# Later maxima for the attention heads, and the weight conversion's integer word in PSUM

## The chip, the cores and the metric

The kernel runs on one core of one Trainium2 chip. The metric is the device time of one execution in microseconds. Three runs of the kernel before gave 982.65, 981.98 and 981.62 us, median 981.98 us. A trace of one execution, taken by the hardware profiler, is the source of every other time in this text. The engines are named as in the profile: PE (TensorE matmul), PEld (its weight load), DVE (VectorE), ACT (ScalarE), POOL (GpSimd), SP (the queue that issues most DMAs).

## The reference

Two layers, one behind the other. The first is attention in which a key counts for a query only if both fall into the same of 64 buckets; the second is a feed-forward layer over the 3072 tokens that the first returns.

```python
# q, k, v: (4, 8, 768, 64); proj: (64, 6)
q_bits = (einsum('bhsd,dk->bhsk', q, proj) > 0)
k_bits = (einsum('bhsd,dk->bhsk', k, proj) > 0)
q_bucket, k_bucket = sum(bits * 2 ** arange(6), -1)
mask   = q_bucket[:, :, :, None] == k_bucket[:, :, None, :]
scores = where(mask, q @ k.T / sqrt(64), -1e9)
attn   = exp(scores - max(scores, -1))
attn   = attn / (sum(attn, -1) + 1e-9)
x      = (attn @ v), as (3072, 512)
# w_in: (512, 2048), w_out: (2048, 512), both float64
h = x @ w_in
g = where(h >= 1, h, where(h <= -1, 0, (h + 1) ** 2 / 4))
out = g @ w_out
```

## The kernel before

The attention takes the 32 heads one after the other, in pairs that share their loads. A head is twelve **units**: two halves of 384 queries, times six blocks of 128 keys. The program writes out units 0 to 383 in one loop over `g`, and each engine works through its own instructions in the order in which that loop issues them; nothing is reordered. What is done beside the units (casts, conversions, transfers) stands in a table `tasks[g]` and is issued at the end of unit `g`. Where this text says "unit 14 of a head" it means unit 2 of the head behind it.

A unit issues, in this order:

- `s_unit(g)`: two matmuls (L371, L372) give the scores of a block, as a sum of a high and a low part, in one of four PSUM buffers of the pool `ps_s`. The mask and the query's maximum are part of the operands: rows 0 to 7 of the tiles `T1` and `T2` hold the bucket bits, and row 7 of one of them holds the negated maximum. ACT takes the exponential twice, once rounded for the matmul (`ph`, L380) and once in full (L385), into the same PSUM buffer, or for key blocks 0 and 3 into SBUF (`pf`).
- the reduction (`max_red`, L314) of the maximum step that was issued at the end of the unit before, if there was one.
- `lo_unit(g - 1)`: the low part `pl` = full minus rounded (L39), for key blocks 0 and 3 on POOL and otherwise on DVE.
- `pv_unit(g - 4)`: three matmuls with the values (L404 to L406) into one of two output banks, `obank[0]` for the first half of the queries and `obank[1]` for the second. Since they lag by four units, `obank[0]` is written in units 4 to 9 of a head and `obank[1]` in units 10 to 15. ACT then copies the bank to SBUF (`xs`, L412).
- a **maximum step** (`max_mm`, L310), if one is due: two matmuls of 128 queries against all keys of a later head, into the one buffer of the pool `ps_m`. Six of them make a head's maxima.
- the tasks of this unit.

The maxima of a head run two heads ahead of it. For heads 6 and up there is one step in each even unit 0, 2, ..., 10 of the head two before; for heads 0 to 5 a table `early` lists the units. When the six are done, `max_clamp` (L342, L344) makes flags and clamps, a PE transposition (`max_tr`, L349) turns the column to a row in `obank[1]`, and `max_put` copies it on ACT (`te`, L354) and sends it by DMA to its row of `T2` (L356) and to DRAM (L357).

In even heads the operands of the next pair but one are prepared: `cast_h` and `low_h` on POOL in units 0 to 3, `move` by DMA, the bucket bits by four matmuls for each half (`bits_mm`, L210) in units 7 (into `obank[1]`) and 11 (into `obank[0]`), a negation on ACT (L216) and a comparison on DVE (`bits_cmp`, L221) in the unit behind each, and `bits_scale` (L273) on POOL.

From head 3 to head 26 one piece of the feed-forward weights is converted in each head from float64 to a high and a low float32 part (`WeightSplit.steps`). Its parts and their units, counted from the head's unit 0:

| part | engine, line | unit |
|---|---|---|
| s0: load of the raw words `wraw` | SP, L62 | 0 |
| s1: square of the high word `wsq` (ACT), exponent and mantissa bits into the word `wa` (DVE) | L69, L70 | 7 |
| s2: sign bits into `wa` | DVE, L74 | 9 |
| s3: low bits into `wa` | DVE, L78 | 13 |
| s4: `wsq` = (square large enough) times `wa` | DVE, L82 | 15 |
| s5, s6, and the store of the sum for odd heads; a store alone for even ones | ACT L87, POOL L39, SP L95 | 17, 19, 21; 16 |

s2 to s4 read `wa`, and s2 and s3 write it in place. `wa` is an SBUF tile with one buffer. The feed-forward layer follows the attention and is not touched by the change.

Of the kernel before, what the change touches and what calls it, by code (L numbers as in the profile page):

```python
# [22 lines left out]
P = 128  # L23
# [18 lines left out]
class WeightSplit:  # L42
# [7 lines left out]
        nc.vector.memset(sc[:, 1:2], 29)  # L50
        self.sc = sc

    def steps(self, src, shape, hi, lo, cp, stage=None, low=None, keep=None):
        nc, n = self.nc, self.n
        st = {}

        def s0():
            st["raw"] = self.pool.tile([P, n, 2], I32, name="wraw")
            dst = st["raw"]
            if len(shape) == 4:  # L60
                dst = dst.rearrange("p (c f) t -> p c f t", c=shape[1])
            nc.sync.dma_start(out=dst, in_=src)  # L62

        def s1():
            raw = st["raw"]
            sq = st["sq"] = self.pool.tile([P, n], F32, name="wsq")
            a = st["a"] = self.pool.tile([P, n], I32, name="wa", bufs=1)
            high = raw[:, :, 1].bitcast(F32)
            nc.scalar.activation(out=sq, in_=high, func=AF.Square)  # L69
            nc.vector.tensor_scalar(out=a, in0=raw[:, :, 1], scalar1=0x07FFFFFF, scalar2=3,  # L70
                                    op0=ALU.bitwise_and, op1=ALU.logical_shift_left)

        def s2():
            nc.vector.scalar_tensor_tensor(out=st["a"], in0=st["raw"][:, :, 1], scalar=self.sc[:, 0:1],  # L74
                                           in1=st["a"], op0=ALU.bitwise_and, op1=ALU.bitwise_or)

        def s3():
            nc.vector.scalar_tensor_tensor(out=st["a"], in0=st["raw"][:, :, 0], scalar=self.sc[:, 1:2],  # L78
                                           in1=st["a"], op0=ALU.logical_shift_right, op1=ALU.bitwise_or)

        def s4():
            nc.vector.scalar_tensor_tensor(out=st["sq"], in0=st["sq"], scalar=WMIN2,  # L82
                                           in1=st["a"].bitcast(F32), op0=ALU.is_ge, op1=ALU.mult)
# [25 lines left out]
POOL_J = (0, 3)  # L109
PV_ORDER = (1, 2, 0, 4, 5, 3)  # L110
NU = 2 * NJ


def attention(ctx, tc, wst, T1, T2, qk, v, pj, cv, x_d, s_d, e_d, tasks, shared):
# [1 line left out]
    const = ctx.enter_context(tc.tile_pool(name="aconst", bufs=1))  # L116
    work = ctx.enter_context(tc.tile_pool(name="awork", bufs=2))
    small = ctx.enter_context(tc.tile_pool(name="asmall", bufs=2))
    shared["work"], shared["small"] = work, small
    ps_s = ctx.enter_context(tc.tile_pool(name="ps_s", bufs=4, space=PSUM))  # L120
    ps_o = ctx.enter_context(tc.tile_pool(name="ps_o", bufs=1, space=PSUM))
    ps_m = ctx.enter_context(tc.tile_pool(name="ps_m", bufs=1, space=PSUM))
# [221 lines left out]
        eng.tensor_scalar(out=nm[:, 0:NJ], in0=nm[:, 0:NJ], scalar1=CLAMP, scalar2=None,  # L344
                          op0=ALU.min)

    def max_tr(hd, bank):
        ps = mx[hd] = obank[bank]
        nc.tensor.transpose(out=ps[0:2 * NJ, 0:P], in_=nms.pop(hd), identity=ident)  # L349

    def max_put(hd):
# [40 lines left out]

    xss = {}

    def pv_unit(n):
        hd, hf, jj = n // NU, (n % NU) // NJ, n % NJ
        j = PV_ORDER[jj]
        pr, h = hd // 2, hd % 2
# [3 lines left out]
        wa = va[:, j, h:h + 2, :].rearrange("p g d -> p (g d)")  # L402
        wb = vb[:, j, h:h + 2, :].rearrange("p g d -> p (g d)")
        nc.tensor.matmul(out=o, lhsT=wa, rhs=ph, start=(jj == 0), stop=False)  # L404
        nc.tensor.matmul(out=o, lhsT=wb, rhs=ph, start=False, stop=False)  # L405
        nc.tensor.matmul(out=o, lhsT=wa, rhs=pl, start=False, stop=(jj == NJ - 1))  # L406
        if jj == NJ - 1:
            if hf == 0:
# [121 lines left out]

    for t in (1, 0):
        at(0, first_scale, 1, t, nc.gpsimd)
    at(9, ones_row, 1, nc.vector)
    at(3, row_clamp, 0, NJ // 2, NJ)
    at(4, row_half, 0, 1, 1)
    for n, g in enumerate((1, 4, 5, 6)):
# [4 lines left out]
        at(8, move, 1, n)  # L541
    at(8, bits_mm, 1, 0, 1)
    at(9, bits_cmp, 1, 0)
    at(9, row_half, 1, 0)
    at(9, row_flags, 0)
    at(10, bits_mm, 1, 1, 0)
# [55 lines left out]
    NG = NH * NU  # L602
    red = None
    early = {}
    for hd, gs in ((0, (0, 2)), (1, (4, 5, 6, 8, 11, 12)), (2, (15, 16, 17, 19, 20, 22)),
                   (3, (21, 23, 24, 26, 27, 29)), (4, (30, 31, 33, 34, 35, 37)),
                   (5, (38, 39, 41, 42, 44, 46))):
        early.update({n: (hd, NJ - len(gs) + i) for i, n in enumerate(gs)})
    for g in range(NG + LAG + 1):
        if g < NG:  # L610
            s_unit(g)
        if red is not None:
            max_red(*red)
            red = None
        if 1 <= g <= NG:
            lo_unit(g - 1)
        if g < 4 * NU:
            due = g in early
            hd, i = early.get(g, (0, 0))
        else:  # L620
            hd, i = g // NU + 2, g % NU // 2
            due = hd < NH and g % 2 == 0
        if g >= LAG and g - LAG < NG:
            pv_unit(g - LAG)
        if due:
            max_mm(hd, 2 * i)
            max_mm(hd, 2 * i + 1)
            red = (hd, i)
        for fn, a in tasks.pop(g, ()):
            fn(*a)  # L630
    for g in sorted(tasks):
        for fn, a in tasks[g]:
            fn(*a)
# [465 lines left out]
def lsh_attn_ffn(ctx: ExitStack, tc: tile.TileContext, qk, v, pj, cv, w_in, w_out, out):  # L1099
# [46 lines left out]
    def conv(g, steps, offs):  # L1146
        for fn, n in zip(steps, offs):
            at(g + n, fn)

    def wi_steps(i, cp, stage=None):  # L1150
        return ws.steps(win_v[:, :, i * P:(i + 1) * P, :], (P, NCT, P, 2), wih[i], wil[i], cp, stage, None, wq[i])

    def wo_steps(i, cp, stage=None, low=None):
        return ws.steps(wout_v[i], (P, DM, 2), woh[i], wol[i], cp, stage, low)
# [21 lines left out]
    attn = {}  # L1176
# [107 lines left out]
```

## Time and profile before

| what | us |
|---|---|
| median of three runs | 981.98 |
| the profiled execution: its span | 980.2 |
| attention: from the first score matmul to the feed-forward layer's first | 12.2 to 463.7 |
| busy PE, DVE, ACT, POOL | 966.7, 793.9, 679.6, 346.3 |

The profiled execution's span runs from its first to its last instruction; the time of a run also holds what lies around it, 1.8 us between this span and the median. In the views, a group's row ends with the time for which the engine stood just before those instructions and what released it, in us. A row of the timeline has the start, the duration, and in brackets the engine's idle time ahead of it. A matmul's row lasts about 0.34 us, but matmuls overlap, and one starts every 0.17 to 0.18 us; so PE's busy time hides short waits, and they are read from the distance of starts.

### The profile page before, as it was taken

Reading aid. Unit: us, or ns where it says so; the run is one execution under the profiler, and the core shown is the slowest. Engines: PE = TensorE matmul, PEld = TensorE weight load, DVE = VectorE, ACT = ScalarE, POOL = GpSimd, SP = SyncE. Lnnn points to the kernel's source line nnn. Section 1 sums busy time; section 2 is a strip of 40 time slices with the busy share of each in tenths; the row PEclk is TensorE's granted clock in tenths of the full one; section 3 lists DMA queues with packets and bytes.
Section 4 is the critical chain, followed back from the end, with each engine's and each line's share of the span. In section 5 each row is a group of like instructions: output and inputs, shape, how many; then the busy total and the mean of one; then the engine's idle time right before and its main releaser. Section 6 shows DMA issues by size and latency. Waiting matters only on the chain.

```text
span 980.2 us, 15590 instructions
## 1 busy us (share of the span) xinstructions
PE 966.7 (99%) x5050; PEld 889.7 (91%) x5050; DVE 793.9 (81%) x1359; ACT 679.6 (69%) x1481; POOL 346.3 (35%) x418
## 2 busy tenths in 40 slices
PE   8999999999999999999999999999999999999998
PEld 7889999999999999999999998888988889988886
DVE  8779999999999999887898887877866777655554
ACT  7878988898899898888655555455564545544444
POOL 8767777778887777666000000000000000000000
PEclk9999999999999999999999999999999999999999
DMA  6674667676666667644395478966458554454431
GB/s 164 178 189 108 165 175 184 192 180 192 168 159 162 177 174 187 161 119 126 126 319 185 129 237 287 314 223 205 116 157 240 149 183 119 143 159 119 117 88 65
DMA packets 95113, 167.56 MB, mean 171 GB/s; under 512 B 13956, under 2 KB 51960, under 8 KB 95032
## 3 DMA queue, kind: packets, MB, share of 16 engines
q1 hardware_dynamic: 94808, 166.56, 59.6%
q8 instruction: 40, 0.66, 0.3%
q14 instruction: 41, 0.34, 0.1%
q10 hardware_dynamic: 224, 0.00, 0.0%
HBM read 106.13 MB, written 33.87 MB: 143 GB/s over the span
## 4 chain that ended last, share of the span: by engine, by line
PE 87%; DVE 5%; ACT 3%; DMA 2%; issue 1%; POOL 1%; SPq 1%; DVEq 0%; ACTq 0%; POOLq 0%
PE y L822 27%; PE h L1054 18%; PE smax L310 7%; PE h L959 7%; PE o L406 5%; PE o L404 5%; PE o L405 5%; PE s L371 5%; PE s L372 5%; DVE nm L314 2%; PE o L210 2%; DVE pl L39 1%; DMA wraw<-in_w_in_dram 1%; ACT ph L380 1%; DMA sm<-sd 0%
## 5 line engine op out<-in xcount | busy, mean ns | idle before, releaser
L380 ACT ACTIVATE ph<-s 128x384 fp32r<-128x384 f32 x380 | 188.3, 496 | 41.1 <-PE s L372 35.1
L314 DVE TENSOR_REDUCE nm<-smax 128x1 f32<-128x768 f32 x189 | 179.0, 947 | 15.2 <-PE smax L310 13.6
L39 POOL TENSOR_TENSOR pl<-pf,ph 128x384 fp32r<-128x384 f32 x128 | 141.9, 1112 | 87.8 <-ACT pf L385 83.1
L787 DVE SCALAR_TENSOR_TENSOR t<-t 128x384 f32<-128x384 f32 x128 | 71.3, 557 | 101.6 <-ACT z L782 101.3
L39 DVE TENSOR_TENSOR pl<-s,ph 128x384 fp32r<-128x384 f32 x256 | 135.8, 544 | 10.8 <-ACT s L385 9.6
L371 PE MATMUL s<-t 128*128 128x384 f32 x384 | 132.2, 344 | 0.0
L404 PE MATMUL o<-ph,va 128*128 128x386 f32 x384 | 130.1, 339 | 1.1 <-DVE neg L221 1.1
L406 PE MATMUL o<-pl,va 128*128 128x386 f32 x384 | 130.1, 339 | 0.4 <-DVE pl L39 0.4
L405 PE MATMUL o<-ph,vb 128*128 128x386 f32 x384 | 130.1, 339 | 0.0
L372 PE MATMUL s<-t 128*128 128x384 f32 x384 | 129.3, 337 | 0.0
L385 ACT ACTIVATE s<-s 128x384 f32<-128x384 f32 x252 | 125.2, 497 | 0.0
L822 PE MATMUL y<-t,ghi 128*128 128x512 f32 x384 | 124.7, 395 | 0.0
L310 PE MATMUL smax<-t 128*128 128x384 f32 x378 | 103.1, 354 | 5.7 <-DVE nm L314 4.4
L781 ACT ACTIVATE t<-h,mh 128x384 f32<-128x384 f32 x56 | 32.6, 581 | 84.0 <-PE h L959 44.3
L310 PEld LDWEIGHTS smax<-t 128*128 128x128 f32 x378 | 64.4, 188 | 23.8 <-DVE nm L314 22.1
L792 ACT CAST ghi<-z 128x384 fp32r<-128x384 f32 x129 | 65.1, 505 | 30.1 <-DVE z L788 26.3
L782 ACT ACTIVATE z<-t,m 128x384 f32<-128x384 f32 x128 | 79.0, 617 | 4.2
L1054 PE MATMUL h<-wbig,t 128*128 128x384 f32 x399 | 81.4, 336 | 0.0
L822 PEld LDWEIGHTS y<-t,ghi 128*128 128x128 f32 x384 | 71.3, 188 | 11.1 <-ACT ghi L792 0.3
L1054 PEld LDWEIGHTS h<-wbig,t 128*128 128x128 f32 x399 | 71.6, 188 | 5.3
L781 ACT ACTIVATE t<-wsq,mh 128x384 f32<-128x384 f32 x48 | 29.6, 617 | 67.0 <-DVE wsq L1067 40.8
L822 PE MATMUL y<-t,glo 128*128 128x512 f32 x192 | 76.0, 396 | 0.0
(189 smaller groups left out, 2134.9 us busy)
## 6 DMA issues: line engine op xcount, KB each, us to landing
t<-wc SPq DMA_DIRECT2D x92, 256.0 KB
t<-t SPq DMA_DIRECT2D x60, 384.0 KB
wraw<-wc SPq DMA_DIRECT2D x76, 256.0 KB
raw<-in_qk_dram SPq DMA_DIRECT2D x14, 768.0 KB
wraw<-in_w_in_dram SPq DMA_DIRECT2D x16, 512.0 KB
wraw<-in_w_out_dram SPq DMA_DIRECT2D x16, 512.0 KB
t<-ed SPq DMA_DIRECT2D x36, 192.0 KB
xd<-xs SPq DMA_DIRECT2D x32, 192.5 KB
```

Of the source, the lines that this page charges most:

```text
L39: eng.tensor_tensor(out=out, in0=a, in1=b, op=ALU.subtract)
L310: nc.tensor.matmul(out=smax[hd][:, hf, 0:HS], lhsT=t2[:, 0, h, i * P:(i + 1) * P], rhs=t2[:, 1, h, hf * HS:(hf + 1) * HS], start=True, sto ...
L314: nc.vector.tensor_reduce(out=nmp(hd)[:, i:i + 1], in_=smax[hd][:, :, 0:HS], axis=AX.XY, op=ALU.max, negate=True)
L371: nc.tensor.matmul(out=ps[:, 0:HS], lhsT=t1[:, 1, h, ks], rhs=t1[:, 0, h, sl], start=True, stop=False)
L372: nc.tensor.matmul(out=ps[:, 0:HS], lhsT=t2[:, 1, h, ks], rhs=t2[:, 0, h, sl], start=False, stop=True)
L380: nc.scalar.activation(out=ph[:, 0:HS], in_=ps[:, 0:HS], func=AF.Exp, scale=SCALE)
L385: nc.scalar.activation(out=pf, in_=ps[:, 0:HS], func=AF.Exp, scale=SCALE)
L404: nc.tensor.matmul(out=o, lhsT=wa, rhs=ph, start=(jj == 0), stop=False)
L405: nc.tensor.matmul(out=o, lhsT=wb, rhs=ph, start=False, stop=False)
L406: nc.tensor.matmul(out=o, lhsT=wa, rhs=pl, start=False, stop=(jj == NJ - 1))
L822: nc.tensor.matmul(out=ys[c][m], lhsT=g_[:, m * P:(m + 1) * P], rhs=w, start=(first and k == 0), stop=(last and k == 2))
L1054: nc.tensor.matmul(out=ps, lhsT=w[:, cs], rhs=x, start=(n == 0 and s not in (2, 3, 6)), stop=(n == 5), skip_group_check=True)
```

## The change

1. **Maxima.** The constant `SHIFT = 4` moves the maximum steps of heads 6 and up four units back, from units 0, 2, ..., 10 to units 4, 6, ..., 14 of the head two before. Their clamp goes from unit 12 to unit 15, the transposition from unit 16 to 17, and the put stays in unit 17. The transposition takes a buffer of `ps_s` instead of `obank[1]`.
2. **Heads 4 and 5.** Their twelve steps were in units 30 to 46, some in neighbouring units. They now stand in units 30 to 50 at nearly even distances, also between two matmuls of a unit: `pv_unit` takes a function `between`, and a key of `early` now counts fifths of a unit. A step that isn't at the end of its unit has its reduction issued right behind it. The steps of heads 0 to 3 stay.
3. **Rows of heads 3, 4 and 5.** Head 3: clamp in unit 30 on POOL (was DVE), transposition and put in unit 33 (were in 31). Head 4: clamp 41 on POOL (was 38 on DVE), transposition and put 43 (were 40 and 41). Head 5: clamp 51, transposition and put 53 (were 48, 52 and 53).
4. **Conversion.** The word `wa` of all conversions in the attention is `obank[0]`, seen as integers, in PSUM. The steps s1 to s4 move from units 7, 9, 13, 15 to 10, 13, 14, 14, and what follows them comes a unit sooner.
5. **Bits.** From the third even head on, the bits' matmuls are in units 5 and 7, both in `obank[1]` (were 7 and 11), with their comparisons, the last move and the scaling behind them. Once, at the start, a memset of a row (`ones_row` of head 1) is issued behind a comparison instead of ahead of it.

```diff
@@ class WeightSplit
-    def steps(self, src, shape, hi, lo, cp, stage=None, low=None, keep=None):
+    def steps(self, src, shape, hi, lo, cp, stage=None, low=None, keep=None, word=None):
...
-            a = st["a"] = self.pool.tile([P, n], I32, name="wa", bufs=1)
+            a = st["a"] = self.pool.tile([P, n], I32, name="wa", bufs=1) if word is None else word()
@@ attention
+SHIFT = 4
...
-    shared["work"], shared["small"] = work, small
+    shared["work"], shared["small"], shared["word"] = work, small, lambda: obank[0].bitcast(I32)
...
-    def max_tr(hd, bank):
-        ps = mx[hd] = obank[bank]
+    def max_tr(hd, bank=None):
+        ps = mx[hd] = ps_s.tile([P, 512], F32, name="s") if bank is None else obank[bank]
...
-    def pv_unit(n):
+    def pv_unit(n, between):
...
         nc.tensor.matmul(out=o, lhsT=wa, rhs=ph, start=(jj == 0), stop=False)
+        between(3)
         nc.tensor.matmul(out=o, lhsT=wb, rhs=ph, start=False, stop=False)
+        between(4)
         nc.tensor.matmul(out=o, lhsT=wa, rhs=pl, start=False, stop=(jj == NJ - 1))
...
-            gc, gt = ((g + NU + 6, g + NU + 7) if hd == 1 else (g + NU + 2, g + NU + 4) if hd == 2
-                      else (g + NU, g + NU + 4))
-            at(gc, max_clamp, hd + 2, nc.gpsimd if hd > 2 else nc.vector)
-            at(gt, max_tr, hd + 2, 1)
-            at(gt + (hd > 1), max_put, hd + 2)
+            gc, gt = ((30, 33), (41, 43))[hd - 1] if hd < 3 else (g + NU + SHIFT - 1, g + NU + SHIFT + 1)
+            at(gc, max_clamp, hd + 2, nc.gpsimd)
+            at(gt, max_tr, hd + 2)
+            at(gt, max_put, hd + 2)
...
-            bits_at = ((20, 1), (23, 0)) if pr == 0 else ((8 if pr == 1 else 7, 1), (11, 0))
+            bits_at = (((20, 1), (23, 0)), ((8, 1), (11, 0)))[pr] if pr < 2 else ((5, 1), (7, 1))
...
-                   (3, (21, 23, 24, 26, 27, 29)), (4, (30, 31, 33, 34, 35, 37)),
-                   (5, (38, 39, 41, 42, 44, 46))):
-        early.update({n: (hd, NJ - len(gs) + i) for i, n in enumerate(gs)})
+        early.update({5 * n + 5: (hd, NJ - len(gs) + i) for i, n in enumerate(gs)})
+    for i in range(2 * NJ):
+        n = 5 * 31 + 35 * i // 4
+        early[n + (n % 5 == 1)] = 4 + i // NJ, i % NJ
+    for hd in range(6, NH):
+        early.update({5 * ((hd - 2) * NU + SHIFT + 2 * i + 1): (hd, i) for i in range(NJ)})
     for g in range(NG + LAG + 1):
+        def between(k):
+            if 5 * g + k in early:
+                hd, i = early.pop(5 * g + k)
+                max_mm(hd, 2 * i)
+                max_mm(hd, 2 * i + 1)
+                if k == 5:
+                    return hd, i
+                max_red(hd, i)
...
         if 1 <= g <= NG:
             lo_unit(g - 1)
+        between(2)
         if g >= LAG and g - LAG < NG:
-            pv_unit(g - LAG)
+            pv_unit(g - LAG, between)
...
+        red = between(5)
         for fn, a in tasks.pop(g, ()):
             fn(*a)
@@ lsh_attn_ffn
-        conv((2 * i + 3) * NU, wi_steps(i, nc.scalar), (0, 7, 9, 13, 15, 17, 19, 21))
+        conv((2 * i + 3) * NU, wi_steps(i, nc.scalar), (0, 10, 13, 14, 14, 16, 18, 20))
...
-        conv((4 + 2 * n) * NU, first, (0, 7, 9, 13, 15, 16))
+        conv((4 + 2 * n) * NU, first, (0, 10, 13, 14, 14, 15))
```

More of the change, by code (lines that the diff above doesn't have):

```diff
@@ L532, in attention @@
         at(0, first_scale, 1, t, nc.gpsimd)
-    at(9, ones_row, 1, nc.vector)
     at(3, row_clamp, 0, NJ // 2, NJ)
@@ L543, in attention @@
     at(9, bits_cmp, 1, 0)
+    at(9, ones_row, 1, nc.vector)
     at(9, row_half, 1, 0)
@@ L604, in attention @@
     early = {}
-    for hd, gs in ((0, (0, 2)), (1, (4, 5, 6, 8, 11, 12)), (2, (15, 16, 17, 19, 20, 22)),
-                   (3, (21, 23, 24, 26, 27, 29)), (4, (30, 31, 33, 34, 35, 37)),
-                   (5, (38, 39, 41, 42, 44, 46))):
-        early.update({n: (hd, NJ - len(gs) + i) for i, n in enumerate(gs)})
-    for g in range(NG + LAG + 1):
+    for hd, gs in ((0, (0, 2)), (1, (4, 5, 6, 8, 11, 12)), (2, (15, 16, 17, 19, 20, 22)), (3, (21, 23, 24, 26, 27, 29))):
+        early.update({5 * n + 5: (hd, NJ - len(gs) + i) for i, n in enumerate(gs)})
[4 more added lines that the diff above has]
+        early.update({5 * ((hd - 2) * NU + SHIFT + 2 * i + 1): (hd, i) for i in range(NJ)})
+    for g in range(NG + LAG + 1):
+        def between(k):
[6 more added lines that the diff above has]
+                max_red(hd, i)
         if g < NG:
@@ L613, in attention @@
             max_red(*red)
-            red = None
         if 1 <= g <= NG:
             lo_unit(g - 1)
[L617 to L622, printed above, removed]
-        if g >= LAG and g - LAG < NG:
-            pv_unit(g - LAG)
[L625 to L628, printed above, removed]
+        between(2)
+        if g >= LAG and g - LAG < NG:
+            pv_unit(g - LAG, between)
+        red = between(5)
         for fn, a in tasks.pop(g, ()):
             fn(*a)
+    assert not early
     for g in sorted(tasks):
@@ L1148, in conv, with word @@
             at(g + n, fn)
+    attn = {}
+    def word():
+        return attn["word"]()
     def wi_steps(i, cp, stage=None):
-        return ws.steps(win_v[:, :, i * P:(i + 1) * P, :], (P, NCT, P, 2), wih[i], wil[i], cp, stage, None, wq[i])
+        return ws.steps(win_v[:, :, i * P:(i + 1) * P, :], (P, NCT, P, 2), wih[i], wil[i], cp, stage, None, wq[i], word)
     def wo_steps(i, cp, stage=None, low=None):
-        return ws.steps(wout_v[i], (P, DM, 2), woh[i], wol[i], cp, stage, low)
+        return ws.steps(wout_v[i], (P, DM, 2), woh[i], wol[i], cp, stage, low, None, None if stage is None else word)
     woh = [hi for hi, lo in wo]
@@ L1175, in lsh_attn_ffn @@
     actx = ExitStack()
-    attn = {}
     for b in range(B - 1):
```

## The prediction

> **What bounds the kernel now.** I read the page first, for the engine that sets the time and for the chain that ends last, then the list of waits.
>
> ```profile
> span 980.2 us, 15590 instructions
> PE 966.7 (99%) x5050; PEld 889.7 (91%) x5050; DVE 793.9 (81%) x1359; ACT 679.6 (69%) x1481; POOL 346.3 (35%) x418
> PE 87%; DVE 5%; ACT 3%; DMA 2%; issue 1%; POOL 1%; SPq 1%; DVEq 0%; ACTq 0%; POOLq 0%
> PEld smax L310 <- DVE nm L314: 22.1, 59, 1.4
> ```
>
> TensorE is the bound, and one thing makes it wait in the attention: the two matmuls of a maximum step (L310) wait until VectorE has reduced the step before (L314), since their PSUM tile has one buffer. What the change can win or lose is that wait. The view by windows sizes it; its columns are length, then busy time and count by engine.
>
> ```profile
> core 0: us, PE busy (x) PEld busy (x) DVE busy (x) ACT busy (x) POOL busy (x), PEclk, DMA share, GB/s
> 46.80:79.80 33.00, 30.49 (x165) 27.66 (x164) 26.65 (x40) 25.36 (x60) 18.20 (x20) 1.00 0.66 170
> 79.80:412.90 333.10, 332.24 (x1850) 318.19 (x1849) 315.15 (x465) 300.38 (x720) 255.60 (x288) 1.00 0.65 172
> 344.72:357.47 12.75, 12.75 (x75) 12.64 (x75) 11.43 (x19) 11.05 (x28) 8.17 (x9) 1.00 0.87 244
> ```
>
> The last window is head 23, which never waits. By the code an odd head issues 73 matmuls (12 units of 5, 12 for maxima, 1 transposition; the row counts two more that reach over its edges): 12.75 / 73 = 0.1747 us each. Heads 4 to 27 (third row) have 12 x (73 + 81) = 1848, an even head adding 8 for its bits: 322.8 us of 333.1, so 10.3 us of standing, 0.43 a head. Heads 2 and 3 (second row) have 163: 28.5 of 33.0, so 4.5 of standing. VectorE is busy 315 of 333 us: nearly full, so order on its queue matters.
>
> **How late a reduction may be.** Rows of the timeline in head 21: three maximum steps on TensorE (units 0, 2 and 4), one exponential on ScalarE, and VectorE between them.
>
> ```profile
> 317.77 0.52 PE L310 MATMUL smax<-t 128*128 128x384 f32 x2
> 319.88 0.51 PE L310 MATMUL smax<-t 128*128 128x384 f32 x2
> 322.17 0.62 PE L310 MATMUL smax<-t 128*128 128x384 f32 x2
> ...
> 319.06 0.49 ACT L385 ACTIVATE s<-s 128x384 f32<-128x384 f32 x1
> ...
> 318.33 0.96 DVE L314 TENSOR_REDUCE nm<-smax 128x1 f32<-128x768 f32 x1 [0.16 <-PE smax L310]
> 319.20 1.58 DVE L78 SCALAR_TENSOR_TENSOR wa<-wraw,wsc,wa 128x512 int32<-128x512 int32 x1
> 320.70 0.55 DVE L39 TENSOR_TENSOR pl<-s,ph 128x384 fp32r<-128x384 f32 x1
> 321.17 0.94 DVE L314 TENSOR_REDUCE nm<-smax 128x1 f32<-128x768 f32 x1
> 322.04 0.54 DVE L39 TENSOR_TENSOR pl<-s,ph 128x384 fp32r<-128x384 f32 x1
> ```
>
> A reduction can begin 0.56 after its step (318.33 - 317.77). It holds VectorE 0.87 (to 319.20). The next step starts 0.06 after its end (321.17 + 0.94, then 322.17). Undisturbed, steps stand 12 matmuls apart: 2.10. So a reduction that begins later than about 2.10 - 1.00 = 1.10 after its step stops TensorE. Here one began at 321.17, 1.29 late, and the next step came at 2.29: 0.19 lost, and 0.10 more because its second matmul follows late (x2 takes 0.62, not 0.52). Between the two reductions VectorE needed 2.84: reduction, one conversion step (L78) stretched to 1.58, one subtraction (0.47, 320.70 to 321.17).
>
> **Heads 4 to 27: what the move of the conversion costs.** Now the four VectorE steps of a head's conversion are issued in four units (7, 9, 13, 15), so at most one falls between two reductions. After, step 1 is issued in unit 10, step 2 in 13, steps 3 and 4 both in 14. The shift by four units is even, so a maximum step stays at the end of every even unit, unit 14 (unit 2 of the next head) included, and its reduction is queued at the start of unit 15, behind all tasks of 14. Between the reductions of units 12 and 14 VectorE must then do: reduction, step 2, subtraction, step 3, step 4.
>
> The price of a step. Rows grouped over heads 4 to 27, and then over 484 to 545 us, where GpSimd is idle:
>
> ```profile
> L39 DVE TENSOR_TENSOR pl<-s,ph 128x384 fp32r<-128x384 f32 x192 | 101.1, 542 | 4.5 <-ACT s L385 4.5
> L78 DVE SCALAR_TENSOR_TENSOR wa<-wraw,wsc,wa 128x512 int32<-128x512 int32 x24 | 27.2, 1135 | 0.0
> L82 DVE SCALAR_TENSOR_TENSOR wsq<-wsq,wa 128x512 f32<-128x512 f32 x24 | 25.7, 1071 | 0.0
> L74 DVE SCALAR_TENSOR_TENSOR wa<-wraw,wsc,wa 128x512 int32<-128x512 int32 x24 | 25.2, 1050 | 0.0
> ...
> L74 DVE SCALAR_TENSOR_TENSOR wa<-wraw,wsc,wa 128x512 int32<-128x512 int32 x8 | 6.0, 752 | 0.3
> L78 DVE SCALAR_TENSOR_TENSOR wa<-wraw,wsc,wa 128x512 int32<-128x512 int32 x8 | 6.0, 745 | 0.0
> L82 DVE SCALAR_TENSOR_TENSOR wsq<-wsq,wa 128x512 f32<-128x512 f32 x8 | 5.5, 692 | 0.4
> L70 DVE TENSOR_SCALAR wa<-wraw 128x512 int32<-128x512 int32 x8 | 3.4, 419 | 0.0
> L857 DVE TENSOR_TENSOR pcs<-pcs 128x384 f32<-128x384 f32 x3 | 1.7, 552 | 0.0
> ```
>
> Steps 2 to 4 read two SBUF operands and take 1.05 to 1.14 us beside a busy GpSimd, 0.69 to 0.75 beside an idle one. The subtraction pl<-s,ph has one operand in PSUM and isn't stretched (542 ns in 192). No row shows a step with its word in PSUM. I take the undisturbed prices, because pl is the nearest row; from below the bound is L70's 419 ns, from above the stretched means. An instruction starts 0.08 before the end of the one ahead of it (322.04 against 322.11), but 0.03 after it if it reads its result (55.82 + 0.87, then 56.72, below). So step 2 is 0.67, the subtraction 0.47, step 3 with step 4 waiting on it 0.78, step 4 0.61, and with the reduction 3.40. The subtraction's operand is ready early enough (319.06 + 0.49 is 1.78 after its head's unit-0 step; step 2 ends at 2.10).
>
> The reduction of unit 12 begins 0.56 to 0.65 late (the square of the new unit 10 holds ScalarE, and so a subtraction ahead of it). That of unit 14 then begins 0.6 + 3.40 - 2.10 = 1.90 after its step, the step of unit 16 at 2.90: 0.80 lost, with the 0.10 for its second matmul 0.90. (TensorE would wait there anyway: the first value matmul of unit 16 writes the bank that holds the word, and step 4 ends after its turn.) The rest of the head has room: step 1 alone in unit 10, and the eight bit matmuls in units 5 and 7 lengthen units with no step in them. I count no other standing there. Clusters follow the conversions of heads 3 to 26; the first falls on wider steps. So 23 x 0.90 = 20.7 us in place of 10.3: **+10.4**. That VectorE as a whole has some 1 us a head less to do doesn't help, since the steps meet in one place.
>
> [...]
>
> **Heads 2 and 3.** Steps of heads 4 and 5 now sit in neighbouring units. Timeline, TensorE and then VectorE:
>
> ```profile
> 58.05 0.62 PE L310 MATMUL smax<-t 128*128 128x384 f32 x2 [1.06 <-DVE nm L314]
> ...
> 61.06 0.51 PE L310 MATMUL smax<-t 128*128 128x384 f32 x2
> 62.62 0.62 PE L310 MATMUL smax<-t 128*128 128x384 f32 x2 [0.16 <-DVE nm L314]
> ...
> 55.82 0.87 DVE L342 TENSOR_SCALAR nm<-nm 128x6 f32<-128x6 f32 x1
> 56.72 0.41 DVE L344 TENSOR_SCALAR nm<-nm 128x6 f32<-128x6 f32 x1
> ```
>
> Neighbours are 7 matmuls (1.22) apart and need 1.56 (61.06 to 62.62): 0.34 + 0.10 lost. There are five such (units 34, 35, 38, 39, 42), and unit 31 loses 1.34, since head 3's clamps (L342, L344) hold VectorE ahead of its reduction. After, the steps are 10 to 12 matmuls apart (1.75 to 2.10 against 1.56) and the clamps are on GpSimd: 1.34 + 5 x 0.44 = **-3.5**. Steps set between value matmuls may still lose a few tenths, as a subtraction of 0.47 can stand ahead of a reduction. The neighbours of units 29 and 30 stay.
>
> **Head 3's row** is transposed in unit 33 instead of 31 and needed by unit 36.
>
> ```profile
> 58.51 0.27 PE L349 MATMUL o<-ident,nm 128*12 128x128 f32 x1
> 58.82 0.26 ACT L354 CAST te<-o 12x128 fp32r<-12x128 f32 x1 [1.45 <-PE o L349]
> 59.10 0.77 SPq L356 DMA_DIRECT2D t<-te  x1
> ...
> 0.72 0.41 ACTq L461 DMA_DIRECT2D pj_raw<-in_pj_dram  x1
> 3.48 0.41 ACT L483 CAST pw<-pj_raw 64x6 fp32r<-64x6 f32 x2 [0.83 <-DMA pj_raw<-in_pj_dram]
> ```
>
> From the transposition to the issue it is 0.59; another transfer of 3 KB landed 2.7 after its issue: 3.3, or 3.8 behind ScalarE's exponentials. TensorE gets there after 18 matmuls (two units, a step, four bit matmuls): 3.14. So 0.2 to 0.7 once, **+0.4**. A transposition now takes a score buffer of four, whose last reader is three units back: hidden, as is step 1 in PSUM (0.4 to 0.75 in a unit where VectorE has no subtraction). From head 4 on rows have six units or more.
>
> **Sum.** 10.4 - 3.5 + 0.4 = +7.3. The profiled span is 980.2; the runs' median, 981.98, holds 1.8 more around it, which stays. 981.98 + 7.3 = **989.3 us**.
>
> **Rivals.**
> - *Cheap words (faster).* If a step on a PSUM word costs what pl holds VectorE, 0.47, the three make 1.41 instead of 2.06, the loss is 0.25, 5.8 for 23, and the whole -4.5 - 3.5 + 0.4 = -7.6: 974.4. At L70's price (0.34 each) nothing is lost: 968.6. It decides below a loss of (10.3 + 3.5 - 0.4) / 23 = 0.58 a cluster, steps of about 0.58. For it: pl is never stretched. Against: it has 384 columns, the steps 512, and no 512-column row with two tensors is under 0.69.
> - *No change.* Steps at 0.60 each without the wait between 3 and 4, and the earlier start 0.56: 0.56 + 0.87 + 0.47 + 1.80 - 2.10 + 1.00 - 2.10 + 0.10 = 0.60, 13.8 in all: 982.4.
> - *The word stays stretched (slower).* If PSUM doesn't free the steps of GpSimd, they hold 0.97, 1.17 and 0.99: the loss is 2.0 a cluster, 46, and the time 1014. pl's 542 speaks against it.
> - *GpSimd is late (slower).* The clamp now stands behind three of the four cast-and-subtract pairs of an even head, and the transposition in unit 5 waits for it. GpSimd's groups in heads 4 to 27:
>
> ```profile
> L39 POOL TENSOR_TENSOR pl<-pf,ph 128x384 fp32r<-128x384 f32 x96 | 108.6, 1137 | 59.1 <-ACT pf L385 58.7
> L39 POOL TENSOR_TENSOR t<-raw,t 128x384 fp32r<-128x384 f32 x48 | 48.9, 1018 | 3.9
> L152 POOL CAST t<-raw 128x384 fp32r<-128x384 f32 x48 | 30.0, 625 | 0.0
> ```
>
> Three pairs (4.9), one subtraction (1.1) and the clamp (0.5) end some 6.5 after the head's begin; the transposition's turn is after units 0 to 5, three steps and the loss of 0.9, 36 matmuls or 7.2: 0.7 of room. Each us beyond it, in 12 heads, would add up to 12.
>
> **How the numbers follow.** Forecast 0.62, its own range 985 to 994 (a loss of 0.77 to 1.1); cheap words 0.19; no change 0.12; the two dear ones 0.07. From 976 to 996 leaves out about half of the cheap case and most of the dear ones. A measurement of this kernel tells 0.2%, 2 us, from no change: slower 0.69, same 0.12, faster 0.19.
>
> **What would show it.** Right: the three steps back to back with one subtraction, 0.7 each whatever GpSimd does; the reduction behind them some 1.9 after its maximum; TensorE standing 0.8 to 0.9 before the maximum of unit 4 of each head from 5 to 27, and nowhere else in them; units 31 to 42 without standing; a short wait at unit 36. Wrong: steps under 0.6, steps still near 1.1, waits on the transposition, or a reduction issued ahead of step 3.

## The result and the profile after

The changed kernel takes 991.62 us (median of four runs, 990.4 to 992.55) against 982.32 us for the kernel before beside it (981.62 to 983.72): a ratio of 1.0091 with a 95% interval of 1.0079 to 1.0104, so 9.3 us slower. The profiled execution has a span of 989.9 us, 9.7 more than before.

The page of the changed kernel, its span, busy times and the shares of the chain that ended last:

```profile
span 989.9 us, 15570 instructions
PE 967.3 (98%) x5050; PEld 889.2 (90%) x5050; DVE 778.7 (79%) x1355; ACT 681.4 (69%) x1481; POOL 318.6 (32%) x422
PE 73%; DVE 11%; ACT 7%; issue 3%; DMA 3%; POOL 2%; SPq 0%; DVEq 0%; POOLq 0%
```

TensorE has the same 5050 matmuls and nearly the same busy time (966.7 us before). VectorE does 15 us less (793.9 before) and GpSimd 28 us less, yet VectorE's share of the chain rose from 5% to 11%: less work, but more of it in TensorE's way. The list of waits shows which (engine, operation, line, its releaser; then us in total, times, longest us):

```profile
PEld smax L311 <- DVE nm L315: 13.6, 35, 0.7
PE o L405 <- DVE wsq L82: 9.4, 24, 1.1
```

The wait of a maximum step for a reduction went down from 22.1 us (59 times) to 13.6 (35 times). New are 24 waits of a value matmul (L405) for step 4 of a conversion (L82), one for each conversion in heads 3 to 26. The view by windows sizes the stretches; first the kernel before (heads 0 and 1, heads 28 to 31), then the changed one (heads 0 and 1, 2 and 3, 4 to 27, 28 to 31). Columns as in the prediction.

```profile
12.22:46.80 34.58, 31.50 (x170) 27.25 (x169) 27.41 (x45) 27.66 (x65) 28.71 (x42) 1.00 0.63 160
412.90:463.70 50.80, 50.03 (x281) 48.27 (x281) 43.26 (x71) 43.68 (x106) 32.59 (x34) 1.00 0.49 136
```

```profile
12.36:46.20 33.84, 31.56 (x171) 27.16 (x170) 27.56 (x45) 27.48 (x65) 28.45 (x42) 1.00 0.64 160
46.20:78.30 32.10, 28.60 (x160) 27.15 (x159) 22.42 (x34) 25.18 (x59) 19.45 (x25) 1.00 0.70 174
78.30:422.60 344.30, 334.70 (x1850) 318.25 (x1850) 303.42 (x465) 302.40 (x721) 226.57 (x287) 1.00 0.63 166
422.60:473.80 51.20, 50.56 (x285) 48.91 (x284) 43.93 (x73) 43.92 (x106) 32.64 (x34) 1.00 0.50 135
```

| stretch | before | after | difference |
|---|---|---|---|
| up to the first score matmul | 12.22 | 12.36 | +0.1 |
| heads 0 and 1 | 34.58 | 33.84 | -0.7 |
| heads 2 and 3 | 33.00 | 32.10 | -0.9 |
| heads 4 to 27 | 333.10 | 344.30 | +11.2 |
| heads 28 to 31 | 50.80 | 51.20 | +0.4 |
| the rest of the span: the feed-forward layer | 516.5 | 516.1 | -0.4 |

The loss is in heads 4 to 27, and it is regular. With 0.1747 us for each of the 1848 matmuls there, TensorE stood 21.5 us there, against 10.3 before. Reckoned in the same way from the start of one head to that of the next, heads 5 to 27 stand 0.80 to 0.85 each (three of them 1.14 to 1.17), and head 4 stands 1.42. The timeline in head 21 shows one such place, three of TensorE's rows and then VectorE:

```profile
325.96 0.51 PE L311 MATMUL smax<-t 128*128 128x384 f32 x2
328.01 0.41 PE L405 MATMUL o<-ph,va 128*128 128x386 f32 x1 [0.32 <-DVE wsq L82]
328.79 0.62 PE L311 MATMUL smax<-t 128*128 128x384 f32 x2
...
324.40 0.96 DVE L315 TENSOR_REDUCE nm<-smax 128x1 f32<-128x768 f32 x1
325.28 0.74 DVE L74 SCALAR_TENSOR_TENSOR o<-wraw,wsc,o 128x512 int32<-128x512 int32 x1
325.93 0.55 DVE L39 TENSOR_TENSOR pl<-s,ph 128x384 fp32r<-128x384 f32 x1
326.40 0.74 DVE L78 SCALAR_TENSOR_TENSOR o<-wraw,wsc,o 128x512 int32<-128x512 int32 x1
327.18 0.69 DVE L82 SCALAR_TENSOR_TENSOR wsq<-wsq,o 128x512 f32<-128x512 f32 x1
327.79 0.95 DVE L315 TENSOR_REDUCE nm<-smax 128x1 f32<-128x768 f32 x1
```

Between the reductions at 324.40 and 327.79 VectorE never pauses: 3.39 us of work, where TensorE brings a maximum every 2.10. The second reduction begins 1.83 after its step (325.96). The value matmul that writes `obank[0]` again waits for step 4, the last reader of the word; the next maximum then still waits for the reduction. The standing is 0.47 at the one, 0.28 at the other and under 0.1 besides.

### The profile page after: what moved, and what is told of

Read it like the earlier page. It is cut to its first block, busy times and chain, and to the rows that moved or that the text cites. A ratio compares the mean times of both kernels' runs of the same rounds, so it can differ in the third digit from the quotient of the medians.

```text
span 989.9 us, 15570 instructions
## 1 busy us (share of the span) xinstructions
PE 967.3 (98%) x5050; PEld 889.2 (90%) x5050; DVE 778.7 (79%) x1355; ACT 681.4 (69%) x1481; POOL 318.6 (32%) x422
## 4 chain that ended last, share of the span: by engine, by line
PE 73%; DVE 11%; ACT 7%; issue 3%; DMA 3%; POOL 2%; SPq 0%; DVEq 0%; POOLq 0%
PE y L829 26%; PE h L1061 18%; PE h L966 7%; PE smax L311 4%; PE o L405 3%; PE o L409 3%; PE s L373 3%; PE o L407 3%; PE s L372 3%; DVE nm L315 3%; ACT ph L381 3%; DVE pl L39 2%; PE o L211 2%; ACT s L386 2%; DVE o L78 2%
## 5 line engine op out<-in xcount | busy, mean ns | idle before, releaser
L39 POOL TENSOR_TENSOR pl<-pf,ph 128x384 fp32r<-128x384 f32 x128 | 130.8, 1022 | 94.1 <-ACT pf L386 94.0
L39 DVE TENSOR_TENSOR pl<-s,ph 128x384 fp32r<-128x384 f32 x256 | 138.0, 549 | 23.5 <-ACT s L386 15.4
L405 PE MATMUL o<-ph,va 128*128 128x386 f32 x384 | 131.7, 343 | 9.4 <-DVE wsq L82 9.4
L311 PE MATMUL smax<-t 128*128 128x384 f32 x378 | 100.5, 347 | 2.9 <-DVE nm L315 2.4
L405 PEld LDWEIGHTS o<-ph,va 128*128 128x128 f32 x384 | 72.0, 187 | 16.4 <-ACT pf L386 11.5
L311 PEld LDWEIGHTS smax<-t 128*128 128x128 f32 x378 | 66.3, 188 | 14.6 <-DVE nm L315 13.6
```

Source lines behind the costliest of these rows:

```text
L39: eng.tensor_tensor(out=out, in0=a, in1=b, op=ALU.subtract)
L311: nc.tensor.matmul(out=smax[hd][:, hf, 0:HS], lhsT=t2[:, 0, h, i * P:(i + 1) * P], rhs=t2[:, 1, h, hf * HS:(hf + 1) * HS], start=True, sto ...
```

## The experiments

Edits are on the changed kernel unless something else is said. "Standing" is read as above, from the same stretch.

**1. The word back in SBUF, the conversion in its old units.** Bits and maxima stay as changed.

```diff
-            a = st["a"] = self.pool.tile([P, n], I32, name="wa", bufs=1) if word is None else word()
+            a = st["a"] = self.pool.tile([P, n], I32, name="wa", bufs=1)
...
-        conv((2 * i + 3) * NU, wi_steps(i, nc.scalar), (0, 10, 13, 14, 14, 16, 18, 20))
+        conv((2 * i + 3) * NU, wi_steps(i, nc.scalar), (0, 7, 9, 13, 15, 17, 19, 21))
...
-        conv((4 + 2 * n) * NU, first, (0, 10, 13, 14, 14, 15))
+        conv((4 + 2 * n) * NU, first, (0, 7, 9, 13, 15, 16))
```

> The changed kernel with the conversion undone: its word is the SBUF tile again and its steps are back in units 7, 9, 13, 15. Cluster theory (the loss comes from steps 2, 3 and 4 standing between two reductions): no period holds two steps, so heads 4 to 27 stand about 0.3 to 0.5 us each as before the change, not 0.84, and the time falls by some 9 to 12 us to 980 to 983. Rival 1 (the later maxima, or the bits in units 5 and 7, cost the time): it stays at 988 or more. Rival 2 (a word in the output bank costs by the bank's handover): the same 980 to 983, so this run tells only rival 1 apart.

Measured: 998.99 us, ratio 1.0167 (1.0146 to 1.0189). A miss: slower than the change itself. Heads 4 to 27 last 351.2 us. All odd heads but one stand 1.6 to 1.75 us, each before one maximum. The timeline of this kernel there, VectorE's step 2 and GpSimd around it:

```profile
352.55 0.97 POOL L274 TENSOR_SCALAR bits<-neg,cvt 32x768 fp32r<-32x768 f32 x1
353.45 2.56 DVE L74 SCALAR_TENSOR_TENSOR wa<-wraw,wsc,wa 128x512 int32<-128x512 int32 x1
353.50 1.00 POOL L39 TENSOR_TENSOR vb<-vraw,va 128x384 fp32r<-128x384 f32 x1
354.47 1.00 POOL L39 TENSOR_TENSOR pl<-pf,ph 128x384 fp32r<-128x384 f32 x1
```

The bits' new units bring GpSimd's scaling and value split in front of a step 2 that reads two SBUF operands, and with the next subtraction behind them GpSimd's instructions stand back to back: step 2 lasts through two of them, 2.56 us where it takes 0.75 beside an idle GpSimd. I had taken the bits' units to be neutral, and with the word in SBUF they aren't. So this run says nothing of the cluster; number 5 takes the bits back too.

**2. The word in SBUF, the new units kept.** Only the first of the three lines above (`a = ...`) is edited.

> The changed kernel with its steps in units 10, 13, 14, 14, but the word in the SBUF tile. Cluster theory: the three steps still stand between the same two reductions and are stretched by GpSimd again (means of 1.05 to 1.14 us in place of 0.69 to 0.75), so TensorE loses 1.2 to 2.0 us a head before the maximum of unit 4 and the time rises to 1000 to 1018. Rival 2 (the bank's handover is the cost): nothing waits for the word any more, and the time falls to 980 to 984.

Measured: 1016.54 us, ratio 1.0343 (1.0327 to 1.0359), as expected. With the word in SBUF no value matmul writes over it, and still heads 10 to 19 stand 1.6 to 2.1 us each, nearly all before a maximum. The odd heads from 5 to 27 show the cluster by itself, since steps 2 to 4 aren't stretched there: 0.74, 0.74 and 0.69 us in each. VectorE in head 13, with a reduction at 221.44, step 2 at 222.30 and a subtraction ahead of these rows, and then TensorE's next maximum:

```profile
223.43 0.74 DVE L78 SCALAR_TENSOR_TENSOR wa<-wraw,wsc,wa 128x512 int32<-128x512 int32 x1
224.20 0.69 DVE L82 SCALAR_TENSOR_TENSOR wsq<-wsq,wa 128x512 f32<-128x512 f32 x1
224.81 0.95 DVE L315 TENSOR_REDUCE nm<-smax 128x1 f32<-128x768 f32 x1
225.81 0.62 PE L311 MATMUL smax<-t 128*128 128x384 f32 x2 [0.66 <-DVE nm L315]
```

Between the reductions lie 3.37 us, as in the changed kernel (3.39), and by the distances of starts TensorE loses 0.82 to 0.87 before the maximum of unit 4 of these heads and 0.10 behind it, though no value matmul waits for the word: the loss doesn't need the handover of the bank. The four steps in the changed kernel, the word in PSUM:

```profile
L74 DVE SCALAR_TENSOR_TENSOR o<-wraw,wsc,o 128x512 int32<-128x512 int32 x24 | 17.9, 746 | 0.0
L78 DVE SCALAR_TENSOR_TENSOR o<-wraw,wsc,o 128x512 int32<-128x512 int32 x24 | 17.9, 745 | 0.0
L70 DVE TENSOR_SCALAR o<-wraw 128x512 int32<-128x512 int32 x24 | 16.7, 695 | 4.7 <-ACT xs L415 4.6
L82 DVE SCALAR_TENSOR_TENSOR wsq<-wsq,o 128x512 f32<-128x512 f32 x24 | 16.5, 686 | 0.8
```

From PSUM steps 2 to 4 last in every head what they last undisturbed (the longest 0.748, 0.747 and 0.689 us). From SBUF their means over the same 24 conversions are 0.857, 0.776 and 0.954 us, and with 0.74, 0.74 and 0.69 in the odd heads some 0.97, 0.81 and 1.22 are left for the even ones. Step 1, the cheapest undisturbed (0.42), is stretched most (1.69 in the mean), and it stands in unit 10, outside the cluster; behind it the odd heads stand 0.5 to 1.1 more at an earlier maximum. So most of the 25 us over the changed kernel are the stretched steps', and the unstretched cluster costs with its word in SBUF about what it costs in PSUM.

**3. The cluster spread.** Step 2 goes from unit 13 to 11, step 3 from 14 to 13; the word stays in PSUM.

```diff
-        conv((2 * i + 3) * NU, wi_steps(i, nc.scalar), (0, 10, 13, 14, 14, 16, 18, 20))
+        conv((2 * i + 3) * NU, wi_steps(i, nc.scalar), (0, 10, 11, 13, 14, 16, 18, 20))
...
-        conv((4 + 2 * n) * NU, first, (0, 10, 13, 14, 14, 15))
+        conv((4 + 2 * n) * NU, first, (0, 10, 11, 13, 14, 15))
```

> The changed kernel with one number moved: step 2 in unit 11 instead of 13, the word still in the output bank, steps 3 and 4 in 13 and 14. Cluster theory: between the reductions of units 12 and 14 stand now two steps, the reduction of unit 12 begins some 0.4 us later, and the loss falls from 0.84 to 0.35 to 0.6 us a head: 982 to 987. Rival 2 (handover, or a price of the word in PSUM itself): steps 3 and 4 and the bank's turn are where they were, 989 to 992.

Measured: 984.92 us, ratio 1.0019 (1.001 to 1.0029), as expected: 6.7 us come back from two numbers. Heads 4 to 27 last 336.7 us. VectorE between two reductions there, a subtraction of 0.55 left out:

```profile
319.96 0.95 DVE L315 TENSOR_REDUCE nm<-smax 128x1 f32<-128x768 f32 x1
320.82 0.75 DVE L78 SCALAR_TENSOR_TENSOR o<-wraw,wsc,o 128x512 int32<-128x512 int32 x1
...
321.94 0.68 DVE L82 SCALAR_TENSOR_TENSOR wsq<-wsq,o 128x512 f32<-128x512 f32 x1
322.54 0.95 DVE L315 TENSOR_REDUCE nm<-smax 128x1 f32<-128x768 f32 x1
```

The steps cost what they did (0.75 and 0.68); between the reductions lie 2.58 us in place of 3.39. The reduction of unit 14 begins 1.5 late in place of 1.83, and most heads stand 0.47 to 0.55 in place of 0.80 to 0.85. Number of instructions, engines and prices are the same, only the order differs: 7.6 of the 11.2 us that heads 4 to 27 had lost are the order's alone. Two of the three steps still stand between two reductions, and this run leaves open what the rest would be without them.

**4. Without the shift of the maxima.** `SHIFT = 0`, and heads 4 and 5 in their old units.

```diff
-SHIFT = 4
+SHIFT = 0
...
-    for i in range(2 * NJ):
-        n = 5 * 31 + 35 * i // 4
-        early[n + (n % 5 == 1)] = 4 + i // NJ, i % NJ
+    for hd, gs in ((4, (30, 31, 33, 34, 35, 37)), (5, (38, 39, 41, 42, 44, 46))):
+        early.update({5 * n + 5: (hd, i) for i, n in enumerate(gs)})
```

> The changed kernel with the maxima of heads 4 and up back in their old units (shift 0; heads 4 and 5 in the units of before), conversion, bits and transposition as changed. Cluster theory: a shift by four is even, so the reductions stand to the steps as before and the heads lose the same 0.84; heads 2 and 3 get back some 2 us of standing between neighbours: 991 to 995. Rival 1 (the later maxima cost): 981 to 984.

Measured: 991.38 us, ratio 1.0086 (1.0069 to 1.0103), as expected. Heads 4 to 27 last 341.8 us and stand 0.73 to 0.82 each (heads 10, 18 and 26 0.92 to 0.94). Moving the maxima by an even number of units changes little for the cluster: it meets another head's maximum in the same unit. The 2.5 us less there go back in heads 2 and 3 (33.9 in place of 32.1) and 28 to 31 (52.3 in place of 51.2).

**5. Maxima alone.** The word in SBUF and the conversion in its old units as in number 1, and the bits back in theirs; later maxima, rows and the order of the memset stay.

```diff
-            bits_at = (((20, 1), (23, 0)), ((8, 1), (11, 0)))[pr] if pr < 2 else ((5, 1), (7, 1))
+            bits_at = ((20, 1), (23, 0)) if pr == 0 else ((8 if pr == 1 else 7, 1), (11, 0))
```

> The changed kernel with conversion and bits as before (word in SBUF, units 7, 9, 13, 15; bits in units 7 and 11 of banks 1 and 0); only the maxima, the rows and the small order at the start remain. If the later maxima are harmless by themselves: heads 4 to 27 stand some 10 us in all as before (7 to 14), heads 2 and 3 gain 3.5 and lose about as much to head 3's row: 979 to 985. If they cost, or if GpSimd's new order stretches a step as in the run with the word in SBUF and early bits: 988 or more.

Measured: 980.96 us, ratio 0.9981 (0.9971 to 0.9991), as expected. The conversion and bits together cost the change 991.62 - 980.96 = 10.7 us; the rest of it gains 1.6. Against number 1 it differs by the bits' units alone: 18 us, by the odd heads' standing of 1.6 to 1.75 there, behind a step 2 of up to 2.58 us. Heads 4 to 27 last 332.9 us. One row of its timeline:

```profile
307.76 0.28 PE L350 MATMUL s<-ident,nm 128*12 128x128 f32 x1 [0.23 <-POOL nm L345]
```

Odd heads now stand nowhere, but most even ones some 0.65, of it 0.4 before the transposition in unit 5, which waits for GpSimd's clamp (heads 4, 10, 18 and 26 stand 1.0 to 1.4, before maxima): the prediction's rival that GpSimd is late, which the changed kernel's slower even heads cover.

**6. Head 3's row two units sooner.** Transposed in unit 31, clamped on VectorE, as before the change.

```diff
-            gc, gt = ((30, 33), (41, 43))[hd - 1] if hd < 3 else (g + NU + SHIFT - 1, g + NU + SHIFT + 1)
-            at(gc, max_clamp, hd + 2, nc.gpsimd)
+            gc, gt = ((30, 31), (41, 43))[hd - 1] if hd < 3 else (g + NU + SHIFT - 1, g + NU + SHIFT + 1)
+            at(gc, max_clamp, hd + 2, nc.vector if hd == 1 else nc.gpsimd)
```

> The changed kernel with head 3's row as before: clamps in unit 30 on VectorE, transposition and put in unit 31. In the changed kernel TensorE stands 2.7 us at the second score matmul of unit 36 for that row's transfer, and 0.7 us before the transposition. If the late transposition and the transfers queued ahead of it cause that: both go, and the clamps on VectorE cost about 0.6 before one maximum: some 2.5 to 3 us less, 988 to 989.5. If the transfer would be late anyway (rival: the queue is full): the wait at unit 36 stays above 1.5 and the time at 991.

Measured: 990.4 us, ratio 1.0078 (1.0063 to 1.0093); 1.2 us under the changed kernel, where 2 to 3.5 were expected: half right. Rows of the changed kernel's timeline first (GpSimd, TensorE, SP's issues), then of this one's:

```profile
59.26 0.23 POOL L345 TENSOR_SCALAR nm<-nm 128x6 f32<-128x6 f32 x1
59.55 0.28 PE L350 MATMUL s<-ident,nm 128*12 128x128 f32 x1 [0.51 <-POOL nm L345]
57.92 2.43 SPq L164 DMA_DIRECT2D t<-t  x3
60.45 1.54 SPq L357 DMA_DIRECT2D t<-te  x1
65.28 0.44 PE L373 MATMUL s<-t 128*128 128x384 f32 x1 [2.50 <-DMA t<-te]
```

```profile
57.60 1.16 SPq L164 DMA_DIRECT2D t<-t  x2
58.85 1.20 SPq L357 DMA_DIRECT2D t<-te  x1
63.26 0.44 PE L373 MATMUL s<-t 128*128 128x384 f32 x1 [0.76 <-DMA t<-te]
```

The row of 3 KB is there 4.8 us after its issue began in the changed kernel (60.45 to 65.28) and 4.4 here (58.85 to 63.26), not 2.7. Here it left 1.6 sooner, the wait at unit 36 fell from 2.74 to 1.0, and that at the transposition from 0.67 to 0.23; the maxima took 0.3 of it back. Before it on SP's queue stand two or three moves of `t`. That they are why it lands late is the likely reading, but no run took them away.

**7. An odd shift.** `SHIFT = 5`, the steps in units 10, 11, 12 and 14, so that a maximum falls into the odd units.

```diff
-SHIFT = 4
+SHIFT = 5
...
-        conv((2 * i + 3) * NU, wi_steps(i, nc.scalar), (0, 10, 13, 14, 14, 16, 18, 20))
+        conv((2 * i + 3) * NU, wi_steps(i, nc.scalar), (0, 10, 11, 12, 14, 16, 18, 20))
...
-        conv((4 + 2 * n) * NU, first, (0, 10, 13, 14, 14, 15))
+        conv((4 + 2 * n) * NU, first, (0, 10, 11, 12, 14, 15))
```

> The changed kernel with SHIFT = 5 and the steps in units 10, 11, 12, 14, word in the output bank. Maxima then end odd units and reductions begin even ones. Cluster theory: between the reductions of units 9, 11, 13 and 15 stand step 1 and step 2, step 3, step 4 in turn; only the last begins some 1.3 after its maximum, so a head loses about 0.3 in place of 0.84: 977 to 980. Rival (handover of the bank): step 4 is still in unit 14 and ends shortly before the value matmul's turn in unit 16, 985 or more.

Measured: 989.89 us, ratio 1.0059 (1.0039 to 1.0078). A miss in the time, though in the place it was made for the cluster's waits are gone. Windows over heads 4 to 27 and 28 to 31, then three of VectorE's rows and a maximum in head 29:

```profile
80.50:417.60 337.10, 331.82 (x1850) 317.42 (x1849) 294.44 (x465) 301.85 (x722) 226.79 (x287) 1.00 0.63 169
417.60:473.00 55.40, 52.12 (x286) 48.88 (x285) 48.47 (x73) 43.81 (x105) 32.39 (x34) 1.00 0.45 125
```

```profile
438.42 1.27 DVE L89 CAST t<-wsq 128x512 fp32r<-128x512 f32 x1
440.19 1.33 DVE L711 CAST t<-raw 128x384 fp32r<-128x384 f32 x1
441.45 0.94 DVE L315 TENSOR_REDUCE nm<-smax 128x1 f32<-128x768 f32 x1
442.45 0.62 PE L311 MATMUL smax<-t 128*128 128x384 f32 x2 [1.42 <-DVE nm L315]
```

In heads 4 to 27 the waits for a reduction are gone but in heads 4, 10, 18 and 26 (0.4 to 0.7; at most 0.06 in the others), and what stands are 0.2 before the value matmul and, in most even heads, some 0.5 before the transposition that waits for GpSimd: 7.2 us less than the changed kernel. Much of the gain is given back elsewhere. In head 29 casts of 1.3 us that prepare the feed-forward layer now stand between two reductions, the same fault in a new place; heads 28 to 31 take 55.4 us in place of 51.2.

Heads 2 and 3 take 34.4 us in place of 32.1, and that isn't the edit's: up to unit 46 the two kernels issue the same instructions. Head 3's row is waited for 2.7 us, as in the changed kernel. But in unit 30 TensorE also stood 1.7 for a row of head 2, and from 66 to 70 us the granted clock was 0.57 (0.998 in the mean of this execution), where it was 1.00 in the changed kernel: 14 matmuls stand in these 4 us in place of 25, by the distances of their starts some 1.6 lost. This is the profile of the longest of five executions, which spread from 986.35 to 990.98 us.

**8. The odd shift with the row of number 6.** Both edits together.

> Both repairs together: SHIFT = 5, steps in units 10, 11, 12, 14, word in the output bank, head 3's row in units 30 and 31. If the two causes add: the time of the run with SHIFT = 5 alone less 2.5 to 3 us, 974 to 977.5, faster than both kernels. If the row's wait hides in the other: no more than 1 us.

Measured: 986.95 us, ratio 1.0044 (1.0029 to 1.0059), a miss like number 7. In the profile the wait for head 3's row fell from 2.7 to 1.1 us. The median is 2.9 under number 7's, but that this is the row's edit isn't shown: two of number 7's executions (986.35 and 986.94) lie within the range of these (986.24 to 987.78), and no lower clock is in this profile.

**9. The memset's order alone,** on the kernel before: `at(9, ones_row, 1, nc.vector)` moved behind `at(9, bits_cmp, 1, 0)`.

> The kernel before with the one memset of unit 9 (ones_row of head 1) issued behind the comparison of the bits instead of ahead of it, nothing else. If that order alone shortens the start: head 0 lasts about 15.2 us as in the changed kernel, not 16.3, since the comparison no longer waits with it for a later matmul, and the value matmul that follows the bits in their bank isn't held. If the shorter head 0 has another source: 16.0 to 16.4.

Measured: 982.72 us in one run, beside 981.85 for the kernel before (980.93 to 983.38), which tells nothing of less than 2 us; the profile does. VectorE and the value matmul before, then VectorE here:

```profile
24.61 0.70 DVE L191 MEMSET t<- 1x768 f32 x1 [0.19 <-PE smax L260]
25.34 0.55 DVE L221 TENSOR_TENSOR neg<-o,neg 32x384 f32<-32x384 f32 x1
25.94 0.44 PE L404 MATMUL o<-ph,va 128*128 128x386 f32 x1 [1.05 <-DVE neg L221]
```

```profile
24.21 0.54 DVE L221 TENSOR_TENSOR neg<-o,neg 32x384 f32<-32x384 f32 x1
```

The comparison is the last reader of a bank that a value matmul of head 0 waits for, and it comes 1.13 sooner. Head 0 lasts 15.23 us in place of 16.29 (15.18 in the changed kernel), head 1 gives some 0.35 back. So the -0.7 of heads 0 and 1 is this line's.

**10. What is good of it together.** Number 5, with number 6's row, and the transpositions and puts of heads 5 and up one unit later, so that GpSimd's clamp is done.

```diff
-            gc, gt = ((30, 33), (41, 43))[hd - 1] if hd < 3 else (g + NU + SHIFT - 1, g + NU + SHIFT + 1)
+            gc, gt = ((30, 31), (41, 43))[hd - 1] if hd < 3 else (g + NU + SHIFT - 1, g + NU + SHIFT + 2)
```

> The run with the maxima alone (conversion and bits as before), with two places mended: the transposition and put of heads 5 and up one unit later (unit 18 of the head two before), and head 3's row in units 30 and 31 with its clamps on VectorE. In the run with the maxima alone TensorE stands 0.4 us in every even head before the transposition, for GpSimd's clamps, and 2.7 in head 3 for the row. If the clamps are just late, one unit (0.9 to 1.2 us) hides them: 12 x 0.4 = 4.7 less, and 1.2 to 2 for the row: 974 to 976, faster than both kernels. If the wait moves with the transposition (GpSimd still behind), 978 or more.

Measured: 978.63 us, ratio 0.9963 (0.9949 to 0.9977), faster than both kernels, but only part of what was expected. The wait at the transposition is gone in heads 4 to 27, but most of it comes back before maxima: those heads last 331.9 us in place of 332.9, where 4.7 less were expected. Head 3's row is still waited for, 1.46 us, and head 30 stands 1.3, where it stood 0.3 in number 5.

## Why the prediction was right, and where it was off

Forecast were 989.3 us, measured 991.62, inside the range given; the sum was 2 us short in the medians and 2.4 in the spans. (The range's lower end, 985, goes by the same sum with a loss of 0.71 a cluster, not with the 0.77 named beside it.)

| step | forecast | measured |
|---|---|---|
| heads 4 to 27 | +10.4 | +11.2 |
| maxima in heads 2 and 3 | -3.5 | -3.5 |
| head 3's row | +0.4 | +3.4 |
| heads 0 and 1 | not counted | -0.7 |

**Heads 4 to 27: right, by its own steps.** Step 2 was to be 0.67 on the queue, the subtraction 0.47, step 3 with the wait of step 4 0.78, step 4 0.61, the reduction 0.87: 3.40. The starts give 0.65, 0.47, 0.78, 0.61 and 0.88: 3.39. The reduction was to begin 1.90 late and began 1.83 late; 0.90 was to be lost and 0.80 to 0.85 were in most heads. It was also right that a value matmul stands in the same place: it takes 0.47 of the loss, and the two waits share it and don't add up. Numbers 2 to 4 bear the mechanism out: the cluster costs no less where no value matmul waits for the word, spreading its steps takes two thirds of the added loss away, and moving the maxima doesn't.

**What was off there.** The first cluster was said to fall on wider steps and to cost nothing. It cost 1.25, before the value matmul that waits for step 4: with the maxima there a reduction stands between its steps 2 and 3, and wider maxima help the reduction, not the bank. Where the maxima of heads 4 and 5 kept their places (number 4), head 4 stood 0.82, like any other. And heads 10, 18 and 26 stand 0.3 more, which I hadn't counted. In each, VectorE has two more instructions of a batch's end ahead of the cluster (L673 and L674, 0.37 and 0.19 us, three times in heads 4 to 27), which would push its reduction back; no run took them away. With some 0.07 less than forecast in each of the other 20 heads, these come to about the 0.8 that is missing.

**The price of a word in PSUM: right.** Steps 2 to 4 take 0.746, 0.745 and 0.686 us, within 6 ns of the undisturbed SBUF rows (0.752, 0.745 and 0.692). The rival of cheap words is out by it, as is the stretched word.

**Maxima in heads 2 and 3: right.** Before a maximum TensorE stood 4.64 us there and now stands 1.13, by the distances of starts. The stretch also holds four matmuls fewer (0.7; heads 28 to 31 hold four more), and it is still only 0.9 shorter, because of the next point.

**Head 3's row: the mis-sized term.** "From the transposition to the issue it is 0.59; another transfer of 3 KB landed 2.7 after its issue": both numbers came from rows that stood free. Here the transposition first waited for a clamp that GpSimd, with casts and subtractions ahead of it, finished at 59.49 (0.67 of standing), the issue began 0.90 after the transposition, not 0.59, behind three moves whose issue took SP until 60.35, and the landing took 4.8. TensorE was at its matmul 3.07 after the transposition, as forecast (3.14); the row came 5.7 after it. So 2.74 and 0.67 in place of 0.2 to 0.7. The GpSimd queue was weighed for the clamps of heads 5 and up, as a rival, and not for this one.

**Heads 0 and 1.** The moved memset was held for nothing. It had a row in the trace before: a value matmul waited 1.05 for the comparison behind it (number 9).

**GpSimd late.** The transposition of even heads was said to have 0.7 of room, with the loss of 0.9 counted in. It holds in the changed kernel, which has no such wait in heads 4 to 27. Where the cluster's loss is gone it doesn't (numbers 5 and 7): 0.4 to 0.5 in most even heads.

## What to carry to other kernels

An engine that is busy for 88% of a stretch isn't judged by its sum but by the busiest period between two things that another engine waits for: list the instructions queued in that period, add the distances of their starts, and compare with the time in which the other engine comes round. Do the same for each place into which a step is moved (the bank it holds, the head in which another stage begins, the queue in front of a small transfer); numbers 1, 7 and the row of head 3 were lost on the one period that wasn't listed. Less work on an engine brought nothing here, and two steps moved by one and two units were worth 7 us.

## What the hardware showed beyond that

VectorE's step 2 with both operands in SBUF lasted 2.56 us in the rows of number 1, through two GpSimd instructions one behind the other; beside an idle GpSimd (the kernel before, 484 to 545 us) it takes 0.752. Step 1, a single SBUF source, lasted 1.69 us in the mean of number 2 and 0.419 beside an idle GpSimd. VectorE and GpSimd in number 2, in one of the places:

```profile
339.94 2.26 DVE L70 TENSOR_SCALAR wa<-wraw 128x512 int32<-128x512 int32 x1
339.93 1.00 POOL L39 TENSOR_TENSOR vb<-vraw,va 128x384 fp32r<-128x384 f32 x1
340.90 1.01 POOL L39 TENSOR_TENSOR pl<-pf,ph 128x384 fp32r<-128x384 f32 x1
```

Step 1 ends here 0.29 us after the second GpSimd instruction (342.20 and 341.91), and step 2 in number 1 ended 0.54 after its second (356.01 and 355.47): both lasted past more than the one GpSimd instruction that came first. With the word in PSUM neither happened in 24 heads of the changed kernel. In head 20 there, step 3 starts at 311.44 and takes 0.74 us, though a GpSimd subtraction runs from 311.35 to 312.36. Step 2 stays between 0.743 and 0.748 us and step 1 between 0.685 and 0.698, slower than alone in SBUF and steady. Why the steps in SBUF last so long beside GpSimd, no run shows.
